# A gated-MLP and linear-attention mixer: residual rows enter the products through a PSUM bank

## The chip, the cores and the metric

The kernel runs on one core of one Trainium2 chip. The time is that of one execution on the device, in microseconds; of several runs the median is given. A core has TensorE (matrix products, which it writes into the eight banks of PSUM), VectorE, ScalarE and GpSimd (elementwise work; GpSimd does not touch PSUM here), and SyncE, which in this kernel issues every DMA. The profile calls them PE, DVE, ACT, POOL and SP; PEld is TensorE's loading of the stationary operand. Each engine works through its own instructions strictly in the order in which the program wrote them, and waits on semaphores for the others. An instruction that waits therefore holds up everything behind it on its engine.

## What is computed

A sequence of 2048 rows of 512 features goes twice through two residual blocks, A and B, with the same weights both times:

```python
x = x + _A_ref(_layernorm(x), A_wqkv, A_wo)      # linear attention, 32 heads of 16
x = x + _B_ref(_layernorm(x), B_w_in, B_w_sp, B_b_sp, B_w_out)   # gated MLP
x = x + _A_ref(_layernorm(x), A_wqkv, A_wo)
x = x + _B_ref(_layernorm(x), B_w_in, B_w_sp, B_b_sp, B_w_out)
```

In block A, `phi(t) = where(t > 0, t + 1, exp(t)) + 1e-6` is applied to queries and keys; `kv = pk^T v`, `z` is the sum of `pk`, and the output is `(pq kv / (pq z + 1e-6)) wo`. In block B, `z = gelu(x w_in)` with 1792 columns; its first half is multiplied by a gate `w_sp layernorm(second half) + b_sp`, where `w_sp` is 2048 x 2048 and mixes the rows; the product with `w_out` comes last. Everything is float32.

## The kernel before

The 2048 rows are cut into 16 tiles of 128 (`NT = 16`). Every float32 operand of a product is split into a high part and the remainder, `split` (L118 on): `high` (L119) copies on ScalarE to the format TensorE takes, `low` (L122) subtracts on VectorE, and `mm3` (L133 to L135) forms high x high, high x low and low x high, so each product of two tiles is three matmuls. A bank is one tile of 128 x 512 float32. Pages (128 x 512 in SBUF) and banks are handed out by `Slots`, first freed first taken; a new owner waits until the old one's last use is done.

One layer (L = 0, then L = 1) is a chain of stages, and each stage writes its engines' order out by hand:

- **P1**, per tile: layer norm, keys and queries, `phi`, and the sums for `kv`. The last six query tiles are put off (`late`, `late_phi`): their products fill TensorE later. `late_phi` ends with three instructions: two on ScalarE (L327, L328) and one on VectorE (L329).
- **transition**: forms the combined matrix W2 of `kv` and `wo`, and prepares the first query tiles.
- **P2**, in steps s = 1 to 18, one tile further in each step. Step s runs on TensorE, in this order: `c(s-1)`, the product of tile s-1 with W2 (12 matmuls); in the first steps transposes and a put-off query product; `e(s-3)`, the second half of the B input product (24 matmuls of 448 columns); and up to two `f` (12 matmuls each), pieces of the first half, which exist from step 6 on, seven for every four tiles. `c2` adds the result to the residual row tile in SBUF (L618) and takes its statistics (L196, L198 on VectorE; L200, L201, L203 on GpSimd). `c3` stores the row tile (L624), normalises it on ScalarE (L209) and stores the normalised tile for the transposed load of a later step. `a`, `a2` scale the query tiles (L565 on GpSimd, L577 to L586 on VectorE; L240 on ScalarE stores the first ones); `b` and `d` turn tiles into stationary operands; `e2` is the GELU on two half banks (L671), `e3`, `e4` its norm; the GELU of `f` is L692. `w1.piece` splits a weight piece, and in the first layer from step 6 on `sums.tick` adds blocks of `w_sp` on GpSimd (L786), from loads that SyncE issues.
- **P4**: 56 steps of the row-mixing product (L906 to L908), whose results are evacuated with bias and gate; then 16 steps `o(i)`, the product with `w_out` (21 matmuls), the addition of the residual tile (L1001) and its store (L1003). `zsplit(i+2)` prepares the operand two steps ahead. In the first layer `join` puts the start of the next P1 between the `o` steps: row loads, three norms (i = 7, 8, 9), and the key and query weights (i = 10 to 13).

The two additions that the change touches are these:

```python
nc.vector.tensor_add(x, x, self.cb)   # L618, in c2
nc.vector.tensor_add(x, x, b)         # L1001, in o
```

Of the kernel before, what the change touches and what calls it, by code (L numbers as in the profile page):

```python
# [49 lines left out]
            self.free_list.append(n)  # L50


class Sheets:


# [16 lines left out]
def mixer_kernel(ctx: ExitStack, tc: tile.TileContext, x_in, wqkv, wo_d, win1_d, win2_d, wsp_d, bsp_d, wout_d,  # L72
# [9 lines left out]
    pages = Slots(main, "pg", 22)  # L82
    quads = Slots(main, "qd", 6)
    bigs = Slots(main, "bg", 4)
    banks = Slots(psum, "bank", 8)

    PAGE = [P, 512]
    ztile = {}
# [29 lines left out]
    def high(h, src):  # L118
        nc.scalar.activation(h, src, AF.Copy)  # L119
# [8 lines left out]
        else:  # L128
            low(l, src, h)

    def mm3(out, a, b, start, stop):
        (ah, al), (bh, bl) = a, b
        nc.tensor.matmul(out, ah, bh, start=start, stop=False)  # L133
        nc.tensor.matmul(out, ah, bl, start=False, stop=False)  # L134
        nc.tensor.matmul(out, al, bh, start=False, stop=stop)  # L135

    class Weight:

# [79 lines left out]
    def transposes(src):  # L218
        b = banks.get([P, 4, P])
        for c in range(4):  # L220
            nc.tensor.transpose(b[:, c, :], src[:, c * P:(c + 1) * P], ident)
        return b

    class Turn:
# [40 lines left out]
    class P1:  # L265
# [123 lines left out]
        def start(self):  # L389

            self.loadx(0)
            self.loadx(1)
            nc.sync.dma_start(ident, ident_d)
            for w in (self.wk, self.wq):
                for _ in range(4):
                    w.fetch()
            self.loadx(2)
            self.loadx(3)
            nc.sync.dma_start(mask, mask_d)
            m, f = pages.get(PAGE, F32R), pages.get(PAGE)  # L400
            nc.vector.memset(f, 1.0)
            nc.vector.tensor_copy(m, f)
            b = banks.get(PAGE)

            def idle(n):
                for _ in range(n):
                    nc.tensor.matmul(b, ones, m, start=True, stop=True)

            idle(10)
            self.ln_a(0)  # L410
            self.ln_a(1)
            self.ln_b(0)
            self.wk.piece()
            self.T_high(0)
            idle(4)
            banks.put(b)
            pages.put(m, f)
            self.T_low(0)
            self.wk.piece()
            self.ln_b(1)  # L420
            self.wk.piece()
            self.wk.piece()
            self.kb[0] = self.proj(0, self.wk, lambda: self.T(1))
            self.ln_a(2)
            for _ in range(4):
                self.wq.piece()
            self.ln_b(2)
# [51 lines left out]
    def transition(p1, p2):  # L479
        wv, wo = p1.wv, p1.wo  # L480
        zh, zl = pages.get(PAGE, F32R), pages.get(PAGE, F32R)
        za = p1.zacc
        nc.vector.tensor_scalar(za, za, NT * PHI_EPS, None, op0=OP.add)
        split(zh, zl, za, True)
        pages.put(za)
        p1.late()
        p1.wk.free()
        g = (quads.get([P, 4, 512], F32R), quads.get([P, 4, 512], F32R))
        for c in range(4):
            split(g[0][:, c, :], g[1][:, c, :], p1.G[c])  # L490
            banks.put(p1.G[c])
        zb = banks.get(PAGE)
        nc.tensor.matmul(zb, ones, zh, start=True, stop=False)
        nc.tensor.matmul(zb, ones, zl, start=False, stop=True)
        pages.put(zh, zl)
        p2.zbc = pages.get(PAGE)
        nc.scalar.activation(feats(p2.zbc, True), feats(zb, False), AF.Copy)
        banks.put(zb)
        p2.a(0)
        p1.late_phi()  # L500
        p2.win1.fetch()
        p2.win1.fetch()
        p2.zeps = small.tile([P, 32], F32, name="zeps", bufs=1)
        nc.vector.tensor_reduce(p2.zeps, p2.zbc.rearrange("p (h d) -> p h d", d=16), axis=mybir.AxisListType.X,
                                op=OP.add)
        nc.vector.tensor_scalar(p2.zeps, p2.zeps, PHI_EPS, PHI_EPS, op0=OP.mult, op1=OP.add)

        p2.a2_den(0)
        m = pages.get([P, 4, P])
        for q in range(4):  # L510
            b = banks.get([P, P])
            s = slice(q * P, (q + 1) * P)
            for c in range(4):
                mm3(b, (wv.h[:, c, s], wv.l[:, c, s]), (g[0][:, c, s], g[1][:, c, s]), c == 0, c == 3)
            nc.vector.tensor_mul(m[:, q, :], b, mask)
            banks.put(b)
        kvh, kvl = pages.get([P, 4, P], F32R), pages.get([P, 4, P], F32R)
        for q in range(0, 4, 2):
            split(kvh[:, q:q + 2, :], kvl[:, q:q + 2, :], m[:, q:q + 2, :])
        pages.put(m)  # L520
        quads.put(*g)
        wv.free()
        p2.a2_mul(0)
        p2.a(1)
        p1.late()
        p2.a2_den(1)
        p2.W2 = (quads.get([P, 4, 512], F32R), quads.get([P, 4, 512], F32R))
        for q in range(4):
            b = banks.get(PAGE)
            mm3(b, (kvh[:, q, :], kvl[:, q, :]), (wo.h[:, q, :], wo.l[:, q, :]), True, True)  # L530
            split(p2.W2[0][:, q, :], p2.W2[1][:, q, :], b)
            banks.put(b)
            if q == 1:
                p2.b(0)
        pages.put(kvh, kvl)
        wo.free()
        p2.a(2)
        p1.late_phi()
        p2.a2_mul(1)
        p1.late()  # L540
        p2.a(3)
        p2.a2(2)
        p1.late_phi()


    class P2:
        def __init__(self, p1):
            self.L = L = p1.L
            self.p1 = p1
            self.win1, self.win2 = w_in1(), p1.win2  # L550
            self.qturn, self.xturn = Turn(f"qt{L}", range(5), True), Turn(f"yt{L}", range(4))
            self.qp, self.qT, self.x, self.ms, self.xB, self.z, self.zms = {}, {}, {}, {}, {}, {}, {}
            self.fq = deque()
            self.fnext = []

        def loadx(self, i):
            if i < NT:
# [43 lines left out]
        def b_low(self, i):  # L601
# [3 lines left out]
            home.put(b)  # L605
            self.qT[i] = (h, l)

        def c(self, i):
            h, l = self.qT.pop(i)
            b = banks.get(PAGE)  # L610
            for g in range(4):
                mm3(b, (h[:, g, :], l[:, g, :]), (self.W2[0][:, g, :], self.W2[1][:, g, :]), g == 0, g == 3)
            pages.put(h, l)
            self.cb = b

        def c2(self, i):
            x = self.x[i]
            nc.vector.tensor_add(x, x, self.cb)  # L618
            banks.put(self.cb)
            self.ms[i] = stats(x, 1)  # L620

        def c3(self, i):
            x = self.x.pop(i)
            nc.sync.dma_start(xs[2 * self.L + 1, i], x)  # L624
            y = pages.get(PAGE)
            turned = self.xturn.turned(i)
            normalise(feats(y, turned), feats(x, False), self.ms.pop(i))
            pages.put(x)
            self.xturn.store(i, y)
            if i in self.xturn.by_pe:  # L630
                self.xB[i] = y
            else:
                pages.put(y)
# [64 lines left out]

        def run(self, sums):
            w1 = self.win1  # L700
            for s in range(1, NT + 3):
                self.loadx(s + 1)
                self.qturn.load(s + 1)
# [39 lines left out]
                if s >= 3:  # L743
                    self.e(s - 3)
                    self.e2(s - 3)
                    self.e3(s - 3)
                self.f()
                self.f()
                self.fq.extend(self.fnext)
# [60 lines left out]
    class P4:  # L810
# [7 lines left out]
        def __init__(self, p2, sums):  # L818
            self.L = p2.L
            self.p2, self.sums = p2, sums  # L820
            self.raw, self.w, self.z, self.z1, self.x, self.zs = {}, {}, {}, {}, {}, {}
            self.steps = [(p, k) for p in self.ORDER for k in range(HT)]
            self.beta = self.delta = None
            self.wout = {}

        def fetch(self, g):
            if g >= len(self.steps):
# [75 lines left out]

        def acc(self, out, h, l, o, w, j, start, stop):
            m = nc.tensor.matmul
            m(out, h[:, o], w[:, 0, j, :], start=start, stop=False, skip_group_check=True)  # L906
            m(out, h[:, o], w[:, 1, j, :], start=False, stop=False, skip_group_check=True)  # L907
            m(out, l[:, o], w[:, 0, j, :], start=False, stop=stop, skip_group_check=True)  # L908
# [76 lines left out]
        def zsplit(self, i):  # L985
# [5 lines left out]
            split(q[:, 0], q[:, 1], src)  # L991
            self.zs[i] = q

        def o(self, i):
            q = self.zs.pop(i)
            b = banks.get(PAGE)
            for f in range(NF):
                mm3(b, (q[:, 0, f, :], q[:, 1, f, :]), self.wout[f], f == 0, f == NF - 1)
            quads.put(q)
            x = self.x.pop(i)  # L1000
            nc.vector.tensor_add(x, x, b)  # L1001
            banks.put(b)
            nc.sync.dma_start(xs[2 * self.L + 2, i], x)  # L1003
            pages.put(x)
# [3 lines left out]
        def run(self, nxt):  # L1008
# [35 lines left out]
                    self.evac(p)  # L1044
            pages.put(*self.bs)
            self.zsplit(1)
            for i in range(NT):
                self.loadx(i + 2)
                self.o(i)
                self.zsplit(i + 2)  # L1050
                if nxt is not None:
# [67 lines left out]
```

## Time and profile before

| | |
|---|---|
| runs | 1406.6, 1407.32, 1407.64 us; median 1407.32 |
| profiled execution | span 1405.0 us from the first to the last instruction |
| TensorE clock granted | 1.000 over the whole span |
| busy PE / DVE / ACT / POOL | 1392.5 / 902.0 / 572.1 / 405.3 us |

The profile is of one execution, with its own span; the runs' median lies 2.3 us above it. In a timeline row stand the start and the length in us, the engine, the line, the operation, the tile written and the tile read (buffer numbers left out), their shapes and the count; in brackets how long the engine sat idle just before and what released it. Neighbouring rows can overlap a little: an instruction begins while the one ahead drains, and the ends of matmuls are modelled. A row of a waits table gives who waited for whom, the total in us, the number of times and the longest. A row of a group gives the shortest, median and longest duration in ns and when the first and the last began.

### The profile page before, as it was taken

What the parts mean: (1) busy time and instruction counts of PE and PEld (TensorE: products, weight loads), DVE (VectorE), ACT (ScalarE), POOL (GpSimd) and SP (SyncE); (2) the same over time, 40 slices, a digit from 0 to 9 for tenths busy, and PEclk for the clock granted to TensorE, in tenths of its full rate; (3) what the DMA queues carried; (4) which work ended last, traced back from release to release, by engine and by line L of the source; (5) the groups of instructions that cost most, each with busy time, mean ns of one, the idle gap of its engine ahead of it and who ended that gap; (6) DMA issues with size and microseconds to landing.
All of it is one profiled execution on the core that took longest, in us unless ns stands there. A gap on an engine that the chain in (4) does not pass through costs nothing.

```text
span 1405.0 us, 17478 instructions
## 1 busy us (share of the span) xinstructions
PE 1392.5 (99%) x6270; PEld 1161.3 (83%) x6270; DVE 902.0 (64%) x1275; ACT 572.1 (41%) x871; POOL 405.3 (29%) x490
## 2 busy tenths in 40 slices
PE   9999999999999999999999999999999999999998
PEld 7777888888888888888888888888888888888887
DVE  7887786763577665583578867766415466665632
ACT  5665544443332332341357655444333233333420
POOL 3643245544356001041024434432100030022300
PEclk9999999999999999999999999999999999999999
DMA  6742157876897444453645412554335344434432
GB/s 198 236 147 68 53 183 232 267 240 203 309 323 265 129 121 141 159 179 105 225 128 159 127 45 96 179 177 163 114 119 158 105 165 134 130 122 167 152 112 90
DMA packets 142454, 225.68 MB, mean 161 GB/s; under 512 B 11936, under 2 KB 50592, under 8 KB 142368
## 3 DMA queue, kind: packets, MB, share of 16 engines
q1 hardware_dynamic: 142368, 224.57, 49.3%
q8 instruction: 49, 0.80, 0.2%
q14 instruction: 37, 0.30, 0.1%
HBM read 156.63 MB, written 67.90 MB: 160 GB/s over the span
## 4 chain that ended last, share of the span: by engine, by line
PE 77%; DVE 3%; ACT 2%; issue 1%; DMA 1%; POOL 0%; SPq 0%; DVEq 0%; POOLq 0%; ACTq 0%
PE bank L907 13%; PE bank L906 13%; PE bank L908 13%; PE bank L135 13%; PE bank L134 13%; PE bank L133 13%; DVE pg L260 1%; DMA pg<-in_x_dram 1%; DVE pg L341 0%; DVE pg L329 0%; ACT pg L328 0%; ACT pg L327 0%; DVE bg L122 0%; ACT z_q L328 0%; ACT z_q L327 0%
## 5 line engine op out<-in xcount | busy, mean ns | idle before, releaser
L906 PE MATMUL bank<-qd,pg 128*128 128x512 f32 x800 | 311.2, 389 | 0.0
L908 PE MATMUL bank<-qd,pg 128*128 128x512 f32 x800 | 311.2, 389 | 0.0
L907 PE MATMUL bank<-qd,pg 128*128 128x512 f32 x800 | 311.2, 389 | 0.0
L845 DVE TENSOR_TENSOR qd<-qd,qd 128x1024 fp32r<-128x1024 f32 x112 | 153.9, 1374 | 176.7 <-ACT qd L844 176.5
L844 ACT ACTIVATE qd<-qd 128x1024 fp32r<-128x1024 f32 x112 | 118.5, 1058 | 215.7 <-PE bank L908 198.9
L933 POOL TENSOR_TENSOR bg<-bg,pg 128x512 f32<-128x512 f32 x56 | 85.5, 1563 | 409.6 <-DVE bg L960 195.5
L906 PEld LDWEIGHTS bank<-qd,pg 128*128 128x128 f32 x800 | 150.1, 188 | 31.6
L908 PEld LDWEIGHTS bank<-qd,pg 128*128 128x128 f32 x800 | 150.2, 188 | 31.1
L907 PEld LDWEIGHTS bank<-qd,pg 128*128 128x128 f32 x800 | 150.2, 188 | 31.0
L135 PE MATMUL bank<-qd,pg 128*128 128x512 f32 x384 | 150.7, 392 | 2.7 <-DVE pg L122 2.5
L200 POOL TENSOR_SCALAR rs<-mv 128x1 f32<-128x1 f32 x96 | 36.1, 376 | 391.5 <-DVE mv L198 363.6
L209 ACT ACTIVATE pg<-pg,nb,rs 128x512 f32<-128x512 f32 x63 | 51.1, 811 | 181.8 <-POOL nb L203 181.7
L133 PE MATMUL bank<-qd,pg 128*128 128x512 f32 x288 | 112.5, 391 | 1.4 <-ACT pg L119 1.4
L134 PE MATMUL bank<-qd,pg 128*128 128x512 f32 x288 | 112.3, 390 | 0.0
L786 POOL TENSOR_TENSOR pg<-pg,pg 128x512 f32<-128x512 f32 x56 | 80.6, 1439 | 49.1 <-DMA pg<-in_wsp_dram 38.7
L133 PE MATMUL bank<-bg,qd 128*128 128x448 f32 x256 | 94.2, 368 | 0.0
L135 PE MATMUL bank<-bg,qd 128*128 128x448 f32 x256 | 93.7, 366 | 0.1
L134 PE MATMUL bank<-bg,qd 128*128 128x448 f32 x256 | 93.6, 366 | 0.0
L135 PEld LDWEIGHTS bank<-qd,pg 128*128 128x128 f32 x384 | 72.0, 188 | 21.2 <-DVE pg L122 6.5
L135 PE MATMUL bank<-qd,bg 128*128 128x512 f32 x224 | 87.4, 390 | 0.0
L134 PE MATMUL bank<-qd,bg 128*128 128x512 f32 x224 | 87.4, 390 | 0.0
L133 PE MATMUL bank<-qd,bg 128*128 128x512 f32 x224 | 87.2, 390 | 0.0
(128 smaller groups left out, 2630.4 us busy)
## 6 DMA issues: line engine op xcount, KB each, us to landing
qd<-s SPq DMA_DIRECT2D x64, 512.0 KB, 3.4
qd<-in_wsp_dram SPq DMA_DIRECT2D x48, 512.0 KB, 3.8
pg<-x SPq DMA_DIRECT2D x64, 256.0 KB, 3.1
z<-pg SPq DMA_DIRECT2D x56, 256.0 KB, 2.5
pg<-in_wsp_dram SPq DMA_DIRECT2D x56, 256.0 KB, 5.1
s<-pg SPq DMA_DIRECT2D x56, 256.0 KB, 5.1
pg<-z SPq DMA_DIRECT2D x56, 256.0 KB, 5.2
x<-pg SPq DMA_DIRECT2D x48, 256.0 KB, 2.6
```

Source lines behind the costliest of these rows:

```text
L133: nc.tensor.matmul(out, ah, bh, start=start, stop=False)
L134: nc.tensor.matmul(out, ah, bl, start=False, stop=False)
L135: nc.tensor.matmul(out, al, bh, start=False, stop=stop)
L200: nc.gpsimd.tensor_scalar(rs, mv[:, 1:2], LN_EPS, None, op0=OP.add)
L209: nc.scalar.activation(y, x, AF.Identity, bias=nb, scale=rs)
L786: nc.gpsimd.tensor_tensor(t, a, b, op=OP.add)
L844: nc.scalar.activation(w[:, 0], r, AF.Copy)
L845: nc.vector.tensor_sub(w[:, 1], r, w[:, 0].bitcast(F32))
L906: m(out, h[:, o], w[:, 0, j, :], start=start, stop=False, skip_group_check=True)
L907: m(out, h[:, o], w[:, 1, j, :], start=False, stop=False, skip_group_check=True)
L908: m(out, l[:, o], w[:, 0, j, :], start=False, stop=stop, skip_group_check=True)
L933: nc.gpsimd.tensor_tensor(u, u, z1, op=OP.mult)
```

## The change

Before a residual product begins, ScalarE copies the tile of residual rows into a bank (`seed`). The product's first matmul no longer starts the bank afresh (`start=False`), so all matmuls add onto the rows. In P2, `c2` takes the statistics from the bank, `c3` normalises from the bank and then copies the bank back into the row tile on ScalarE, before the tile's store is issued, which moves behind the normalisation. In P4, `o` copies the finished bank into the row tile on ScalarE instead of adding on VectorE.

The seed of P2's tile s is written into ScalarE's order in step s, behind the GELU of `e2(s-3)` and ahead of those of `f`; the seed of tile 0 stands ahead of step 1. In P4 the seed of tile i+1 stands ahead of `o(i)`. A new class `Banks` records how many columns of each bank the last fresh product covered (transposes record 0), and `seeded` takes the first free bank on which a product of that width will add rather than overwrite.

```diff
+class Banks(Slots):
+    def __init__(self, pool, prefix, n):
+        super().__init__(pool, prefix, n)
+        self.adds = [0] * n
+    def started(self, t, columns):
+        self.adds[self.held[id(t)][0]] = columns
+    def seeded(self, shape):
+        for n in self.free_list:
+            if self.adds[n] >= shape[-1]:
+                self.free_list.remove(n)
+                self.free_list.appendleft(n)
+                return self.get(shape)
+        return None
...
-    banks = Slots(psum, "bank", 8)
+    banks = Banks(psum, "bank", 8)
...
-    def mm3(out, a, b, start, stop):
+    def mm3(out, a, b, start, stop, shared=False):
...
+        if start:
+            banks.started(out, out.shape[-1])
...
+        def seed(self, i):
+            if i >= NT:
+                return
+            b = self.cb[i] = banks.seeded(PAGE)
+            high(b, self.x[i])
+
         def c(self, i):
             h, l = self.qT.pop(i)
-            b = banks.get(PAGE)
             for g in range(4):
-                mm3(b, (h[:, g, :], l[:, g, :]), (self.W2[0][:, g, :], self.W2[1][:, g, :]), g == 0, g == 3)
+                mm3(self.cb[i], (h[:, g, :], l[:, g, :]), (self.W2[0][:, g, :], self.W2[1][:, g, :]), False, g == 3,
+                    True)
             pages.put(h, l)
-            self.cb = b
 
         def c2(self, i):
-            x = self.x[i]
-            nc.vector.tensor_add(x, x, self.cb)
-            banks.put(self.cb)
-            self.ms[i] = stats(x, 1)
+            self.ms[i] = stats(self.cb[i], 1)
 
         def c3(self, i):
-            x = self.x.pop(i)
-            nc.sync.dma_start(xs[2 * self.L + 1, i], x)
+            x, b = self.x.pop(i), self.cb.pop(i)
             y = pages.get(PAGE)
             turned = self.xturn.turned(i)
-            normalise(feats(y, turned), feats(x, False), self.ms.pop(i))
+            normalise(feats(y, turned), feats(b, False), self.ms.pop(i))
+            high(x, b)
+            banks.put(b)
+            nc.sync.dma_start(xs[2 * self.L + 1, i], x)
             pages.put(x)
...
         def run(self, sums):
             w1 = self.win1
+            self.seed(0)
             for s in range(1, NT + 3):
...
                     self.e3(s - 3)
+                self.seed(s)
                 self.f()
                 self.f()
...
+        def seed(self, i):
+            if i >= NT:
+                return
+            b = self.ob[i] = banks.seeded(PAGE)
+            high(b, self.x[i])
+
         def o(self, i):
             q = self.zs.pop(i)
-            b = banks.get(PAGE)
+            x, b = self.x.pop(i), self.ob.pop(i)
             for f in range(NF):
-                mm3(b, (q[:, 0, f, :], q[:, 1, f, :]), self.wout[f], f == 0, f == NF - 1)
+                mm3(b, (q[:, 0, f, :], q[:, 1, f, :]), self.wout[f], False, f == NF - 1, True)
             quads.put(q)
-            x = self.x.pop(i)
-            nc.vector.tensor_add(x, x, b)
+            high(x, b)
             banks.put(b)
...
             self.zsplit(1)
+            self.seed(0)
             for i in range(NT):
                 self.loadx(i + 2)
+                self.seed(i + 1)
                 self.o(i)
```

More of the change, by code (lines that the diff above doesn't have):

```diff
@@ L129, in split @@
             low(l, src, h)
-    def mm3(out, a, b, start, stop):
+    def mm3(out, a, b, start, stop, shared=False):
         (ah, al), (bh, bl) = a, b
-        nc.tensor.matmul(out, ah, bh, start=start, stop=False)
-        nc.tensor.matmul(out, ah, bl, start=False, stop=False)
-        nc.tensor.matmul(out, al, bh, start=False, stop=stop)
+        nc.tensor.matmul(out, ah, bh, start=start, stop=False, skip_group_check=shared)
+        nc.tensor.matmul(out, ah, bl, start=False, stop=False, skip_group_check=shared)
+        nc.tensor.matmul(out, al, bh, start=False, stop=stop, skip_group_check=shared)
+        if start:
+            banks.started(out, out.shape[-1])
     class Weight:
@@ L221, in transposes @@
             nc.tensor.transpose(b[:, c, :], src[:, c * P:(c + 1) * P], ident)
+        banks.started(b, 0)
         return b
@@ L415, in start @@
             idle(4)
+            banks.started(b, 512)
             banks.put(b)
@@ L494, in transition @@
         nc.tensor.matmul(zb, ones, zl, start=False, stop=True)
+        banks.started(zb, 512)
         pages.put(zh, zl)
@@ L554, in __init__ @@
             self.fnext = []
+            self.cb = {}
         def loadx(self, i):
@@ L823, in __init__ @@
             self.beta = self.delta = None
-            self.wout = {}
+            self.wout, self.ob = {}, {}
         def fetch(self, g):
@@ L905, in acc @@
             m = nc.tensor.matmul
+            if start:
+                banks.started(out, 512)
             m(out, h[:, o], w[:, 0, j, :], start=start, stop=False, skip_group_check=True)
```

## The prediction

> **What bounds the kernel now.** I read the page's busy line first, then TensorE's table of waits, then the timelines of each engine where the two changed products run.
>
> ```profile
> span 1405.0 us, 17478 instructions
> PE 1392.5 (99%) x6270; PEld 1161.3 (83%) x6270; DVE 902.0 (64%) x1275; ACT 572.1 (41%) x871; POOL 405.3 (29%) x490
> PE bank L135 <- DVE pg L122: 2.5, 4, 0.7
> ```
>
> TensorE is busy for all but 12.5 of 1405.0 us, so its queue is the bound, and the change takes no matmul from it. There is little to win: of its waits, the only one near the change is 2.5 us behind `low` (L122). What matters is whether TensorE must newly wait. The starts of `c(0)` to `c(5)`, the attention output products of the first P2, on TensorE:
>
> ```profile
> 149.64 0.39 PE L133 MATMUL bank<-qd,pg 128*128 128x512 f32 x1
> 152.36 0.60 PE L221 MATMUL bank<-ident,pg 128*128 128x128 f32 x4
> 155.55 0.39 PE L133 MATMUL bank<-qd,pg 128*128 128x512 f32 x1
> 162.92 0.39 PE L133 MATMUL bank<-qd,pg 128*128 128x512 f32 x1
> 172.25 0.40 PE L133 MATMUL bank<-qd,pg 128*128 128x512 f32 x1
> 180.74 0.39 PE L133 MATMUL bank<-qd,pg 128*128 128x512 f32 x1
> 188.86 0.40 PE L133 MATMUL bank<-qd,pg 128*128 128x512 f32 x1
> ```
>
> `c` lasts 2.72 us (149.64 to 152.36); the early steps last 5.91, 7.37, 9.33, 8.49 and 8.12 us. ScalarE in the same stretch:
>
> ```profile
> 152.75 0.58 ACT L327 ACTIVATE z_q<-bank 128x512 f32<-128x512 f32 x1
> 153.36 0.63 ACT L328 ACTIVATE z_q<-z_q 128x512 f32<-128x512 f32 x1
> 153.90 0.58 ACT L119 ACTIVATE pg<-bank 128x512 fp32r<-128x512 f32 x1
> 157.62 0.82 ACT L209 ACTIVATE pg<-pg,nb,rs 128x512 f32<-128x512 f32 x1 [3.14 <-POOL nb L203]
> 159.42 0.64 ACT L240 ACTIVATE pg<-pg 128x512 f32<-128x512 f32 x1 [0.98 <-DVE pg L586]
> 159.96 0.57 ACT L327 ACTIVATE z_q<-bank 128x512 f32<-128x512 f32 x1
> 160.57 0.63 ACT L328 ACTIVATE z_q<-z_q 128x512 f32<-128x512 f32 x1
> 174.78 0.98 ACT L671 ACTIVATE z_z<-bank 128x448 f32<-128x448 f32 x2
> 182.45 0.95 ACT L671 ACTIVATE z_z<-bank 128x448 f32<-128x448 f32 x2
> 191.20 0.82 ACT L209 ACTIVATE pg<-pg,nb,rs 128x512 f32<-128x512 f32 x1 [4.65 <-POOL nb L203]
> 192.95 0.95 ACT L671 ACTIVATE z_z<-bank 128x448 f32<-128x448 f32 x2
> 847.38 0.63 ACT L328 ACTIVATE z_q<-z_q 128x512 f32<-128x512 f32 x1
> ```
>
> The reader is to see that ScalarE runs late: the work it does for step 1 (157.62 to 161.20) ends after TensorE has begun step 2 (155.55). Today nothing on TensorE needs that work soon.
>
> **The change, part by part.** *Removed:* 64 residual adds on VectorE.
>
> ```profile
> L618 DVE TENSOR_TENSOR pg<-pg,bank x32: 640/675/689, 154.6 to 1010.9; 128x512 f32<-128x512 f32 x32
> 156.07 0.18 DVE L198 BATCH_NORM_AGGREGATE mv<-st 128x2 f32<-128x6 f32 x1
> 156.35 0.22 POOL L200 TENSOR_SCALAR rs<-mv 128x1 f32<-128x1 f32 x1 [14.86 <-DVE mv L198]
> 157.32 0.27 POOL L203 TENSOR_SCALAR nb<-mv,rs 128x1 f32<-128x1 f32 x1
> 158.07 1.32 DVE L586 SCALAR_TENSOR_TENSOR pg<-z_q,den 128x512 f32<-128x512 f32 x1
> ```
>
> 32 x 0.675 us here and as many in P4 leave an engine 64% busy; what this gives TensorE is at most the 2.5 us of waits on `low`, queued behind that add. *Added:* 64 seeds and 64 copies back on ScalarE. No row shows ScalarE writing a bank, so a seed is bounded by its 128x512 rows: 0.57 (L327) to 0.82 us (L209). I take 0.6, nearest the plain copies (0.58); back to back they step 0.55, since neighbouring rows overlap by 0.09 (153.99 to 153.90); normalise then counts 0.72. Twelve exposed seeds at 0.82 would add 2.6 us.
>
> [...]
>
> *Statistics and normalise on the bank:* one bank operand instead of one page operand, same shapes; the rows that read a bank (0.57 to 0.58) are no longer than those that read a page (0.63), so 0. *Store of x moved behind normalise and copy back:* on SP's queue the y store behind it goes out about 0.55 (copy) + 0.5 (issue) later. Its reader is the transposed load, used a step later; a step of 8 to 13 us hides 1.05. Without that cover it is a delay of each step, priced under the second rival. *Banks:* one more is held for about a step of eight, and `seeded` takes one free for long: 0.
>
> *The new wait* carries the sum: `c(i)` cannot begin before seed(i), queued on ScalarE behind all of step i's normalise, store, phi and GELU; and what stands behind the seed (the `f` GELUs, the weight copy) is not needed sooner.
>
> - seed(0) stands behind the last `late_phi`, which ends at 153.99. It ends at 154.5, so `c(0)` starts at 154.55 instead of 149.64: **+4.9**.
> - Step 1: `c(0)` ends 157.3; statistics without the add reach the aggregate at 158.1. From there to the end of L586 it was 3.3 us (156.07 to 159.39); `low(1)` now waits for its transposes behind `c(0)`, +0.3: 161.75. POOL's 1.25, normalise and copy back (0.72 + 0.55) fit in before. L240 to the end of L328 is 1.78: 163.55; then the seed. `c(1)` at 164.0 instead of 155.55: **+8.45** in all.
> - Step 2: the same chain of 9.45 with d(0)'s transposes and one more VectorE `low`, +0.8: `c(2)` at 174.25, **+11.3**.
> - Steps 3 and 4: no `f` follows `e`. The seed waits for the second GELU half, which waits for the end of `e`: 8.49 of TensorE work + 0.1 + half a pair of GELUs 0.55 + seed 0.6 = 9.75 each. `c(4)` at 193.75, **+13.0**.
> - Step 5: from the end of step 4's GELUs to normalise it was 7.8 (183.40 to 191.20), less 0.67 for the add; from normalise to the end of the GELUs 2.7 (191.20 to 193.90), plus copy back 0.55 and seed 0.55. From 193.1 that makes `c(5)` 204.1 instead of 188.86: **+15.2**.
>
> The second layer starts the same way at the same spacing (the `exp` ahead of its first seed stands at 847.38, 694.02 after the first layer's), so **2 x 15.2 = 30.4**. From step 6 two `f` products follow `e`, and TensorE covers the chain. In the second layer, between two `c` starts:
>
> ```profile
> 945.47 0.39 PE L133 MATMUL bank<-qd,pg 128*128 128x512 f32 x1
> 951.73 0.82 ACT L209 ACTIVATE pg<-pg,nb,rs 128x512 f32<-128x512 f32 x1 [4.94 <-POOL nb L203]
> 954.00 0.95 ACT L671 ACTIVATE z_z<-bank 128x448 f32<-128x448 f32 x2
> 958.52 0.39 PE L133 MATMUL bank<-qd,pg 128*128 128x512 f32 x1
> ```
>
> GELUs end at +9.48; less 0.7 for the add, plus 0.55 and 0.55, the seed ends at +9.9 of a 13.05 us step: hidden with 3 us to spare. In steps with one `f` (13.05 - 2.72 = 10.33) it just fits; I give the four of them **0.7** together. In the first layer alone, the first matrix sums of step 6 wait for loads that SP issues behind the stores of that step's `f`:
>
> ```profile
> 206.32 1.93 SPq L115 DMA_DIRECT2D pg<-in_wsp_dram  x4
> 212.42 2.65 POOL L786 TENSOR_TENSOR pg<-pg,pg 128x512 f32<-128x512 f32 x2 [3.94 <-DMA pg<-in_wsp_dram]
> ```
>
> The second `f` now ends at +13.05 of the step, its GELU and first store at +14.3; 6.1 later (206.32 to 212.42) come the adds, 2.65 long, then POOL's 1.25 for `c(6)` and from normalise to the seed's end 3.2 + 1.1: +28.6 against the 26.1 at which TensorE wants `c(7)`: **+2.5**.
>
> P4, first layer, where the next P1's norms are joined:
>
> ```profile
> 669.82 0.69 DVE L1001 TENSOR_TENSOR pg<-pg,bank 128x512 f32<-128x512 f32 x1 [3.07 <-PE bank L135]
> 671.42 0.68 DVE L196 BATCH_NORM_STATS2 st<-pg 128x6 f32<-128x512 f32 x1
> 673.69 0.82 ACT L209 ACTIVATE pg<-pg,nb,rs 128x512 f32<-128x512 f32 x1 [21.96 <-POOL nb L203]
> 674.57 0.69 DVE L1001 TENSOR_TENSOR pg<-pg,bank 128x512 f32<-128x512 f32 x1 [2.25 <-PE bank L135]
> 686.39 2.07 SPq L115 DMA_DIRECT2D pg<-in_wqkv_dram  x4
> 691.02 0.63 ACT L119 ACTIVATE qd<-pg 128x512 fp32r<-128x512 f32 x1 [5.23 <-DMA pg<-in_wqkv_dram]
> ```
>
> An `o` takes 4.75 us (669.82 to 674.57). In front of seed(i+2) after `o(i)` now stand the copy back (0.6), the split's copy of 128x896 (about 0.95, by elements from the 128x512 row) and the join's work: alone 2.2, hidden. With a norm: copy 0.6, split copy 0.95, its VectorE `low` (0.9, from the end of L1001 at 670.51 to 671.42), then the chain from statistics to normalise, 671.42 to 673.69 = 2.27, normalise 0.72, seed 0.6, hand-overs 0.15: 6.2. For i = 7 that is 1.45 over; for 8 and 9, whose chain begins right behind the seed before, 1.15 each. At i = 10 the join's copy waits for loads issued behind the x store: 4.63 from issue to use (686.39 to 691.02) after about 1.4 of copy back and issues, then 1.15 for copy and seed, less 4.75: 2.4. Together **+6.2**. The second layer's P4 has no join: 0. The tail changes an add of 0.69 into a copy of 0.6: **-0.1**.
>
> Sum: 30.4 + 0.7 + 2.5 + 6.2 - 0.1 = **39.7 us** on a profiled span of 1405.0. That span lies 2.3 below the runs' median of 1407.32, so the run becomes 1407.3 + 39.7 = **1447** (+2.8%).
>
> **The rivals.** *The TensorE clock drops in the new stalls.* The forecast idles TensorE for about 4.9, 3.3 and 4.1 us at the start of each P2, longer than any wait in this trace after its start. What a slow TensorE looks like stands at the start:
>
> ```profile
> 2.31 4.11 PE L407 MATMUL bank<-pg,ones 128*128 128x512 f32 x10 [2.31 <-DVE pg L402]
> ```
>
> Ten matmuls in 4.11 us, 0.41 each, against 12 in 2.72, 0.227 each; the page's granted clock still reads full there. A relapse costs 10 x 0.18 = 1.8 us; four make 7.3: **1454**. Nothing in the trace shows a relapse, so 0.17. [...]
>
> *The ScalarE chain becomes the period in the first layer's middle.* There VectorE and POOL also work for the sums, and the x page and the y page come free later. At +1.05 per step and nothing hidden in steps 6 to 15, 10 us more: **1457**. Against it: the chain has 3 us to spare once ScalarE waits for TensorE. 0.13.
>
> *Only the relief of VectorE counts.* If every seed were done before TensorE asks, the four waits on `low` (2.5 us) would go and nothing come: **1404.8**, no change by this kernel's measure (0.2%). The place is seed(0): it decides if ScalarE ends the last `late_phi` before 149.6. The rows say 153.99, by the order of its own queue. 0.04; a partial exposure (P4's joins hidden, about 1440) lies inside the forecast.
>
> **How the numbers follow.** Forecast 0.66, clock 0.17, chain 0.13, relief 0.04. The forecast alone: 1436 to 1452 (P4's 6.2 and the sums' 2.5 away, or seeds at 0.82 and 2 to 3 us of longer chains). The range 1431 to 1463 adds both slower rivals and chains 15% shorter. Faster by over 0.2%: 0.02; within: 0.03; slower: 0.95.
>
> **What would show it.** On TensorE: waits released by ScalarE's copy into a bank ahead of `c(0)` to `c(5)`, about 5, 3.5, 4, 1.2, 1.2, 2.5 us in each layer; almost none from `c(8)` on; a few of 1 to 2 us at the ninth to twelfth `o` of the first P4 and none in the second. VectorE about 43 us less busy, ScalarE about 77 more (128 x 0.6). Wrong if ScalarE's early seeds end before TensorE arrives, if `c` starts without them, or if waits persist through the steps with two `f`.

## The result and the profile after

The changed kernel takes 1455.76 us (median of 4 runs, 1455.05 to 1459.02), the kernel before 1407.48 us in the same comparison (4 runs, 1406.6 to 1407.88): a ratio of 1.0349, interval 1.0337 to 1.0361. It is 3.5% slower. The forecast was 1447, the range 1431 to 1463.

In the changed kernel's lines, `high` is L138, `low` L141, `mm3` L152 to L154, the normalisation L230, the transposes L242. The page of the changed kernel, its span, its busy line, its line of granted clock (one digit for each fortieth of the span), and the costliest form of the product's first matmul:

```profile
span 1453.8 us, 17527 instructions
PE 1406.6 (97%) x6270; PEld 1169.4 (80%) x6270; DVE 853.7 (59%) x1211; ACT 637.7 (44%) x999; POOL 405.7 (28%) x490
PEclk9999799999999999999999998999999999999999
L152 PE MATMUL bank<-qd,pg 128*128 128x512 f32 x288 | 118.4, 411 | 33.3 <-ACT bank L138 31.7
```

TensorE issues the same 6270 matmuls and is busy 14.1 us longer (1406.6 against 1392.5); the rest of the 48.8 us by which the span grew is idle time. VectorE is 48.3 us less busy and ScalarE 65.6 us more, against the 43 and 77 of the forecast. (The 128 added copies last 76.0 us one by one; busy time counts the overlap of neighbouring rows only once.) TensorE's table of waits, two rows:

```profile
PE bank L152 <- ACT bank L138: 36.9, 15, 4.7
PE bank L154 <- DVE pg L141: 0.6, 1, 0.6
```

Fifteen times TensorE waits for ScalarE's copy into a bank, 36.9 us in all; the waits on `low` shrank from 2.5 to 0.6. That is 35.0 us more idle, and with the 14.1 us of busy time 49.1, against the 48.8 by which the span grew. The waits on TensorE's timeline, in the first layer's P2, then c(0) to c(2) of the second, then `o(9)` to `o(11)` of the first P4:

```profile
155.06 0.80 PE L152 MATMUL bank<-qd,pg 128*128 128x512 f32 x1 [4.72 <-ACT bank L138]
155.66 0.63 PE L153 MATMUL bank<-qd,pg 128*128 128x512 f32 x1
156.09 0.63 PE L154 MATMUL bank<-qd,pg 128*128 128x512 f32 x1
...
159.93 0.60 PE L242 MATMUL bank<-ident,pg 128*128 128x128 f32 x4
...
167.12 0.80 PE L152 MATMUL bank<-qd,pg 128*128 128x512 f32 x1 [3.85 <-ACT bank L138]
...
179.68 0.62 PE L152 MATMUL bank<-qd,pg 128*128 128x512 f32 x1 [3.13 <-ACT bank L138]
...
191.16 0.50 PE L152 MATMUL bank<-qd,pg 128*128 128x512 f32 x1 [1.13 <-ACT bank L138]
...
201.05 0.50 PE L152 MATMUL bank<-qd,pg 128*128 128x512 f32 x1 [1.13 <-ACT bank L138]
...
211.18 0.50 PE L152 MATMUL bank<-qd,pg 128*128 128x512 f32 x1 [1.77 <-ACT bank L138]
...
698.05 0.50 PE L152 MATMUL bank<-wo,qd 128*128 128x512 f32 x1 [1.43 <-ACT bank L138]
...
704.01 0.50 PE L152 MATMUL bank<-wo,qd 128*128 128x512 f32 x1 [0.91 <-ACT bank L138]
...
711.86 0.50 PE L152 MATMUL bank<-wo,qd 128*128 128x512 f32 x1 [2.79 <-ACT bank L138]
...
877.70 0.79 PE L152 MATMUL bank<-qd,pg 128*128 128x512 f32 x1 [4.73 <-ACT bank L138]
...
890.22 0.79 PE L152 MATMUL bank<-qd,pg 128*128 128x512 f32 x1 [3.87 <-ACT bank L138]
...
901.71 0.50 PE L152 MATMUL bank<-qd,pg 128*128 128x512 f32 x1 [3.43 <-ACT bank L138]
...
902.98 0.39 PE L154 MATMUL bank<-qd,pg 128*128 128x512 f32 x1
903.21 0.39 PE L152 MATMUL bank<-qd,pg 128*128 128x512 f32 x1
```

Two things are to be seen. The brackets are the new waits. And behind `c(0)`'s wait the matmuls start 0.43 us apart (155.66 to 156.09), behind `c(2)`'s in the second layer 0.23 (902.98 to 903.21): `c(0)` now lasts 4.87 us (155.06 to 159.93) where it lasted 2.72. The stretches of the changed kernel's trace (busy time of PE, PEld, DVE, ACT, POOL with their counts; the column before the last two is the granted clock) say why:

```profile
152.00:160.00 8.00, 4.93 (x13) 3.87 (x14) 1.34 (x2) 2.23 (x4) 0.00 (x0) 0.57 0.00 0
160.00:170.00 10.00, 6.15 (x24) 4.73 (x23) 5.05 (x8) 4.64 (x8) 3.57 (x5) 0.81 0.25 79
170.00:180.00 10.00, 6.87 (x28) 5.31 (x27) 4.79 (x9) 4.96 (x9) 2.32 (x4) 0.84 0.23 79
872.00:885.00 13.00, 8.27 (x28) 6.26 (x27) 5.41 (x11) 3.49 (x7) 0.69 (x2) 0.74 0.00 0
```

The clock was granted in full everywhere in the kernel before; here it falls six times: behind `c(0)`, `c(1)`, `c(2)` in the first layer, `c(0)`, `c(1)` in the second, and `o(11)` in the first P4. The two kernels issue the same matmuls in the same order, so the step from each start to the next, less the idle time, can be compared one by one. Of the 14.1 us, 12.3 lie in steps at half clock: some 50 matmuls that start 0.43 instead of 0.23 us after the one ahead, and longer first steps and transposes beside them. Another 1.2 are first steps behind waits that ran at full clock, ten of the fifteen (0.34 instead of 0.23 us). The last 0.7 us is spread over the trace.

### The profile page after: what moved, and what is told of

Same layout as the page of the kernel before. It is cut to its first block, busy times and chain, and to the rows that moved or that the text cites. A ratio compares the mean times of both kernels' runs of the same rounds, so it can differ in the third digit from the quotient of the medians.

```text
span 1453.8 us, 17527 instructions
## 1 busy us (share of the span) xinstructions
PE 1406.6 (97%) x6270; PEld 1169.4 (80%) x6270; DVE 853.7 (59%) x1211; ACT 637.7 (44%) x999; POOL 405.7 (28%) x490
## 4 chain that ended last, share of the span: by engine, by line
PE 81%; ACT 7%; DVE 7%; issue 2%; DMA 2%; POOL 1%; SPq 0%; DVEq 0%; ACTq 0%; POOLq 0%
PE bank L152 14%; PE bank L153 14%; PE bank L154 14%; PE bank L940 12%; PE bank L941 12%; PE bank L939 12%; DVE pg L282 1%; DVE pg L351 1%; ACT pg L230 1%; DVE pg L363 1%; ACT pg L350 1%; ACT z_q L350 1%; ACT pg L349 1%; DVE bg L141 1%; ACT z_q L349 1%
## 5 line engine op out<-in xcount | busy, mean ns | idle before, releaser
L939 PEld LDWEIGHTS bank<-qd,pg 128*128 128x128 f32 x800 | 150.1, 188 | 31.4
L940 PEld LDWEIGHTS bank<-qd,pg 128*128 128x128 f32 x800 | 150.2, 188 | 31.1
L941 PEld LDWEIGHTS bank<-qd,pg 128*128 128x128 f32 x800 | 150.1, 188 | 31.1
L154 PE MATMUL bank<-qd,pg 128*128 128x512 f32 x384 | 153.8, 400 | 0.7 <-DVE pg L141 0.6
L152 PE MATMUL bank<-qd,pg 128*128 128x512 f32 x288 | 118.4, 411 | 33.3 <-ACT bank L138 31.7
L138 ACT ACTIVATE pg<-bank 128x512 f32<-128x512 f32 (+1 forms) x77 | 45.6, 592 | 127.3 <-PE bank L154 91.5
L152 PEld LDWEIGHTS bank<-qd,pg 128*128 128x128 f32 x288 | 56.4, 196 | 50.7 <-ACT bank L138 37.3
L141 DVE TENSOR_TENSOR qd<-bg,qd 128x896 fp32r<-128x896 f32 x32 | 35.8, 1117 | 103.1 <-ACT qd L138 103.1
L152 PE MATMUL bank<-bg,qd 128*128 128x448 f32 x256 | 94.0, 367 | 0.0
L154 PE MATMUL bank<-bg,qd 128*128 128x448 f32 x256 | 93.4, 365 | 0.0
L152 PE MATMUL bank<-wo,qd 128*128 128x512 f32 x224 | 88.1, 394 | 5.1 <-ACT bank L138 5.1
L154 PEld LDWEIGHTS bank<-qd,pg 128*128 128x128 f32 x384 | 74.4, 194 | 18.3 <-DVE pg L141 2.4
```

What stands on the lines that cost most here:

```text
L141: nc.vector.tensor_sub(l, src, h.bitcast(F32))
L152: nc.tensor.matmul(out, ah, bh, start=start, stop=False, skip_group_check=shared)
L154: nc.tensor.matmul(out, al, bh, start=False, stop=stop, skip_group_check=shared)
```

## The experiments

Theory: the seed's place in ScalarE's queue makes TensorE wait (forecast), and the waits cost a second time through the clock (first rival). Other theories: ScalarE's added work costs by itself; the price lies in P4.

**Which product carries it.** Two kernels, each with one half of the change.

```diff
 # p2_only: o(i) and its loop as before; c, c2, c3 as changed
 # p4_only: c, c2, c3 and their loop as before; o(i) as changed
```

> The seeds of P2 alone; P4 adds on VectorE as before. If the time went to TensorE waiting for P2's early seeds and to the slow matmuls behind those waits, this keeps nearly all of it: the changed kernel's 1455.8 us less the 5.1 us of waits at the first P4's o steps, 1450.5 us (1449 to 1452). If P4's copies back cost more than those waits show, it is clearly lower, 1440 or less.

> The seeds of P4 alone; P2 as before. By the waits at three o steps of the first P4 (1.4, 0.9, 2.8 us): 1407.5 + 5.1 = 1412.5 us (1411.5 to 1414), and none of it in the second layer's P4, which has no join. If the copies back on ScalarE cost by themselves, about 0.6 us for each of 32 tiles, it would be 1420 us or more.

The first product alone took 1453.88 us (1447.56 to 1454.05; ratio 1.0316, 1.0293 to 1.0339), the output product alone 1413.75 (ratio 1.0042, 1.0027 to 1.0057). TensorE's waits, of the first:

```profile
PE bank L152 <- ACT bank L138: 31.6, 12, 4.7
```

and of the second:

```profile
PE bank L152 <- ACT bank L138: 4.8, 3, 2.4
```

The twelve waits are `c(0)` to `c(5)` in two layers, the three are `o(9)` to `o(11)`. Both halves came out above the expected 1450.5 and 1412.5 us, by 3.4 and 1.3 us, and together they cost 53.0 us where the whole change costs 48.3. The number of falls of the clock differs: the trace of the first half has seven in P2, that of the changed kernel five.

**The clock by itself.** The same kernel as the changed one, but TensorE does useless matmuls while it would wait.

```diff
         def c(self, i):
+            if i < 3:
+                self.fill((18, 14, 14)[i])   # matmuls into a bank that nobody reads
```

> The changed kernel with 18, 14 and 14 extra matmuls on spare data ahead of c(0), c(1) and c(2) of each layer, into a bank that nothing reads; they run while TensorE waits for the seed. If the slow matmuls (0.43 us apart instead of 0.23) come of the clock after an idle stretch, they go: c(0) to c(3) take about 29.7 us in each layer instead of 36.1 and 33.9, and the time is about 1445 us (1443 to 1448) with a granted clock near 1.00. If they are slow because they add onto a bank that ScalarE wrote, or share a port with it, nothing changes: 1455 us or, with the extra work, more.

It took 1445.7 us (1444.76 to 1447.95; ratio 1.0271, 1.0256 to 1.0286): 10.1 us faster than the changed kernel, with 92 matmuls more. Its timeline and its stretch around `c(0)`:

```profile
149.52 4.24 PE L642 MATMUL bank<-qd 128*128 128x512 f32 x18
154.41 0.50 PE L152 MATMUL bank<-qd,pg 128*128 128x512 f32 x1 [0.64 <-ACT bank L138]
```

```profile
155.00:165.00 10.00, 9.31 (x43) 7.40 (x42) 5.06 (x8) 4.66 (x8) 2.30 (x4) 1.00 0.22 79
```

`c(0)` still starts at 154.4 and not at 149.6, so the wait is there, filled; the clock is full. `c(0)` to `c(5)` start at 154.41, 164.50, 174.58, 184.46, 194.34 and 204.48 us. The 10.1 us is the share of the clock; the 12.3 counted above are of one execution, and the four runs of each of the two kernels spread over 4.0 and 3.2 us. What is left, 1445.7 - 1407.3 = 38.4 us, is the waits and the restarts behind them.

**ScalarE's work without the wait.** The kernel before, with all 128 additional ScalarE copies at their places, the seeds into a bank that nobody reads and the copies back into a spare page; VectorE still adds.

```diff
         def c2(self, i):
             nc.vector.tensor_add(x, x, self.cb)
...
             normalise(feats(y, turned), feats(x, False), self.ms.pop(i))
+            g = pages.get(PAGE)
+            high(g, self.cb)
...
+                self.seed(s)
```

> The kernel before, with all of ScalarE's added work and none of the new order on TensorE: at each place of a seed ScalarE copies the rows into a bank that nothing reads, at each place of a copy back it copies the product's bank into a spare page; the products start afresh and VectorE still adds. If the cost is the wait for the seed, the time stays near 1407.5 us (1406 to 1411) with ScalarE some 77 us busier. If it is ScalarE's 128 extra copies by themselves, or their access to the banks, it is about that of the changed kernel, 1450 us.

1417.56 us (ratio 1.0069, 1.0052 to 1.0086): a miss, 10 us above the kernel before. Its waits and the longest of them:

```profile
PE bank L133 <- ACT qd L119: 3.6, 5, 1.9
```

```profile
695.51 0.50 PE L133 MATMUL bank<-wo,qd 128*128 128x512 f32 x1 [1.87 <-ACT qd L119]
```

No product waits for a seed, but the copies hold up others of ScalarE's work: the high parts of operands (`qd`) come late five times, and behind the last, in the first P4, the clock falls once more. Compared step by step with the kernel before, TensorE is idle for 5.1 us more, the slow stretch costs 1.6 and the first steps behind waits 1.2; some 2 of the 10.2 us by which the span grew are not explained. So ScalarE's work is not free where its place in the queue is ahead of an operand. Whether it costs anywhere else, the next runs tell.

**The seeds one tile earlier.** In P2 seed(s+1) in step s, the first two ahead of the last `late_phi`; in P4 seed(i+2) right behind the copy back of `o(i)`. One kernel does both, one only P2.

```diff
+        p2.seed(0)
+        p2.seed(1)
         p1.late_phi()
...
-            self.seed(0)
...
-                self.seed(s)
+                self.seed(s + 1)
...
+            self.seed(1)             # this and the next two only in the first of the two kernels
...
-                self.seed(i + 1)
                 self.o(i)
+                self.seed(i + 2)
                 self.zsplit(i + 2)
```

> The changed kernel with every seed one tile earlier in ScalarE's order: P2's seeds of tiles 0 and 1 in the transition, ahead of the second put-off phi, then the seed of tile s+1 in step s; P4's seed of tile i+2 right behind the copy back of o(i), ahead of the split and the join. All work of the change is kept. If the wait for late seeds (and the clock behind it) is the whole cost, the waits by ScalarE's copy into a bank vanish, VectorE's relief takes back some of the 2.5 us of waits on its low parts, and the time is about 1405 us (1404 to 1409), no slower than before. If statistics, normalise and copies on the bank cost by themselves, it stays above 1420.

> The same with P4's seeds left where the change has them. Expected: the 5.1 us of waits at the first P4 return, about 1410 us (1409 to 1414); the difference to the run before prices P4's place alone.

Both early: 1425.56 us (ratio 1.0123, 1.0105 to 1.0141), far from the expectation. P2 alone early: 1415.97 (ratio 1.0059, 1.0043 to 1.0075), at 2 us above its range. On ScalarE, in the kernel with both, two neighbouring instructions:

```profile
695.85 0.60 ACT L138 ACTIVATE bank<-pg 128x512 f32<-128x512 f32 x1 [6.76 <-DMA pg<-x]
696.39 0.94 ACT L138 ACTIVATE qd<-bg 128x896 fp32r<-128x896 f32 x1
```

and on its TensorE:

```profile
697.38 0.80 PE L152 MATMUL bank<-wo,qd 128*128 128x512 f32 x1 [6.07 <-ACT qd L138]
```

A seed put earlier asks for the residual row earlier. This one sat 6.76 us at the head of ScalarE's queue waiting for the row's load, the split behind it came late, and TensorE waited 6.07 us for the split. The wait was moved from one operand to another.

**P2 early, P4 as before.** This asks whether place in the queue is all that the change costs in P2.

```diff
 # as the kernel with P2 early; o(i) adds on VectorE again, no seeds in P4
```

> The first product with its seeds one tile earlier (as in the run with the first product's seeds early), the output product as in the kernel before. In that earlier run the stalls of the first product were gone but for 0.90, 0.62 and 0.90 us, against 0.72, 0.56, 0.72 and 0.55 us before, so if place in ScalarE's queue is all that the change costs there, 1407.5 us (1406 to 1409.5). If ScalarE's added work costs by itself what the run with the work and without the wait lost, shared evenly between the two products, 1411 to 1413. If the freed VectorE shortens anything, under 1405.

1408.26 us (10 runs, 1407.39 to 1410.88), against 1407.33 (19 runs): ratio 1.0009, interval 1.0 to 1.0019. The busy line of its page, and two rows of its TensorE's waits:

```profile
PE 1393.2 (99%) x6270; PEld 1162.0 (83%) x6270; DVE 878.2 (62%) x1243; ACT 603.0 (43%) x935; POOL 406.9 (29%) x490
```

```profile
PE bank L152 <- ACT qd L138: 1.9, 1, 1.9
PE bank L154 <- DVE pg L141: 1.8, 2, 0.9
```

There is no row for a copy into a bank any more. ScalarE does all 64 added copies of P2, VectorE is 23.8 us less busy, and TensorE's time is what it was. Some 46 us of the 48 of the change are the place of P2's seeds in one queue. What the relief of VectorE gives is not seen by itself: the waits on `low` shrink from 2.5 to 1.8 us, a new wait of 1.9 us on an operand of ScalarE's (`qd`) stands against it, and the net is no gain.

**P4's seeds out of the way.** The seed of tile i+2 behind the split of tile i+2 and ahead of what `join` issues; in a second kernel the residual row is also loaded one tile earlier. P2 early in both.

```diff
-                self.loadx(i + 2)
-                self.seed(i + 1)
+                self.loadx(i + 2)        # second kernel: i + 3
                 self.o(i)
                 self.zsplit(i + 2)
+                self.seed(i + 2)
```

> Both seeds off the path: the first product's one tile earlier, the output product's tile i+2 seeded behind the split of tile i+2 and ahead of what the next layer puts in, so that no normalisation stands between a seed and its product and no load held by a seed stands ahead of a split. Place in the queue as the whole cost: the three stalls of 1.44, 0.91 and 2.42 us at the first output product go, and with the last one its half-clock stretch of some 1.9 us; from 1415.97 us that gives 1409.3 (1407 to 1411). If a seed that waits for its residual load only moves the stall (it held ScalarE 6.76 us when it stood ahead of the split), a wait of 2 us or more on a ScalarE copy stays and the time is 1413 to 1418.

> As the run with the seed behind the split, with the residual row of the output product loaded one tile earlier as well. If the residual's load is what is late, this is the fastest of the three with no wait on ScalarE at the first output product: 1408.5 us (1406.5 to 1411). If the load was not late there, no difference from that run beyond 1 us. If the third residual page starves another tile of pages, a wait on a load appears and the time is over 1412.

The first took 1414.74 us (ratio 1.0056, 1.0041 to 1.0071), the second 1410.15 (ratio 1.0022, 1.0013 to 1.0032). In the first the seed's load moved the stall, as its second expectation had it; ScalarE there:

```profile
689.01 0.60 ACT L138 ACTIVATE bank<-pg 128x512 f32<-128x512 f32 x1 [6.07 <-DMA pg<-x]
```

TensorE waited 4.20 us behind it. With the load one tile earlier that is gone, and what is late next shows; ScalarE and TensorE of the second kernel:

```profile
693.91 0.63 ACT L138 ACTIVATE qd<-pg 128x512 fp32r<-128x512 f32 x1 [3.81 <-DMA pg<-in_wqkv_dram]
...
696.40 0.50 PE L152 MATMUL bank<-wo,qd 128*128 128x512 f32 x1 [1.75 <-ACT bank L138]
```

The join's copy of a weight piece waits 3.81 us for its load, the seed stands behind it, and TensorE idles 1.75 us. No version with seeds was faster than the kernel before.

**How short a wait costs the clock.** The rows of P4 had shown half clock behind waits of 1.75 to 2.8 us. So the full fill was cut, to leave idle time of that length ahead of `c(0)` to `c(2)`.

```diff
-                self.fill((18, 14, 14)[i])
+                self.fill((9, 6, 4)[i])      # fill_half;  (13, 9, 8) in fill_most
```

> The change with 9, 6 and 4 matmuls into an unread bank ahead of c(0), c(1) and c(2) of each layer, in place of 18, 14 and 14. Waits and fill together are as long as with the full fill, so all time above that run's 1445.7 us is clock. The remaining idle is 2.65, 2.5 and 2.5 us (the full fill's remainder plus 9, 8 and 10 matmuls of 0.2275 us). Theory A, half clock only after some 3 us of idle or more: no relapse in P2 and 1445.7 (1444.5 to 1447.5). Theory B, idle of 1.75 to 2.8 us is enough when its phase is bad, as the rows of the first output product in four kernels suggest: two to six relapses of some 1.9 us in P2, 1449 to 1457.

> As before with 13, 9 and 8 matmuls: idle of 1.75, 1.8 and 1.6 us remains ahead of c(0), c(1) and c(2). Theory A: 1445.7 us (1444.5 to 1447.5). Theory B: between the full and the half fill, up to four relapses, 1446 to 1452; the waits of 1.71 to 1.77 us at c(5) in the changed kernel left the clock full, so fewer relapses than with the half fill.

1449.92 us (1446.79 to 1453.22; ratio 1.0291, 1.0274 to 1.0309) and 1447.82 us (1446.79 to 1450.39; ratio 1.0287, 1.0271 to 1.0302): above the 1445.7 of the full fill though the same time is waited or filled. The intervals of the three ratios overlap, so the times alone do not decide; the granted clock does. It was 0.998 to 0.999 in the four runs of the full fill and 0.993 to 0.997 in those of the half fill. In P2, where no wait of the two kernels is longer than 2.7 us, the traces show four falls with the half fill, three with the larger one and none with the full fill: theory B holds. TensorE's timeline of the first, and its stretches around those rows (why they are cut at these times is told in the last section):

```profile
154.51 0.80 PE L152 MATMUL bank<-qd,pg 128*128 128x512 f32 x1 [2.69 <-ACT bank L138]
...
178.72 0.50 PE L152 MATMUL bank<-qd,pg 128*128 128x512 f32 x1 [2.52 <-ACT bank L138]
```

```profile
150.38:153.79 3.41, 1.44 (x7) 0.86 (x5) 1.62 (x4) 2.08 (x4) 0.00 (x0) 1.00 0.00 0
153.79:157.21 3.42, 2.69 (x6) 2.17 (x7) 0.69 (x1) 0.67 (x2) 0.00 (x0) 0.50 0.00 0
174.27:177.69 3.42, 1.92 (x9) 1.27 (x7) 1.99 (x4) 2.25 (x5) 0.93 (x1) 1.00 0.46 135
177.69:181.10 3.41, 2.38 (x10) 1.99 (x11) 0.69 (x1) 1.53 (x3) 1.29 (x1) 1.00 0.28 100
```

Half clock came behind 2.69 us of idle and not behind 2.52: of the first wait 1.97 us lie in one stretch of 3.41 us, of the second 1.50 and 1.03 us in two.

## Why the prediction was right, and where it was not

The sign, the place and the mechanism were right. The time came out 8.8 us above the forecast because one rival happened beside it; the stated range had room for that. Term by term:

- *The waits at `c(0)` to `c(5)`.* The forecast named about 5, 3.5, 4, 1.2, 1.2 and 2.5 us; measured were 4.72, 3.85, 3.13, 1.13, 1.13, 1.77 in the first layer and 4.73, 3.87, 3.43 at the start of the second. The forecast's 30.4 us for both layers stands against 15.7 + 16.0 of waits less the 1.9 saved on `low`: 29.8. The per-step chain that set them (GELU half, normalise, copy back, seed) was read correctly from the rows of before. The kernel with the stalls filled, where the clock stays full, shows it best: `c(1)`, `c(2)`, `c(4)` and `c(5)` start at 164.50, 174.58, 194.34 and 204.48 us, and the forecast put them at 164.0, 174.25, 193.75 and 204.1. (The six waits that the forecast lists as signs come to 17.4 us a layer, its own starts move by 15.2; the measured 15.7 and 16.0 lie nearer the starts.)
- *The clock in the new stalls* is what the forecast left out of its sum. It was a rival at 0.17 with 4 events of 1.8 us, 7.3 in all; that there would be four was the author's estimate, which no run shows. It came six times and cost 10 to 12 us (10.1 by the full fill, 12.3 counted in one trace). The forecast's reason, that nothing in the trace shows a relapse, was worth little: after its start the longest wait in the trace of before is 1.36 us (at 41.24 us), and the shortest that half clock followed, in the traces counted in the last section, is 1.75 us. (Nor does the full clock that its page gives for the slow first matmuls say anything: that trace's first record of the clock begins at 5.65 us.) Forecast 39.7 and clock 10.1 would be 49.8; measured 48.3. That these lie so close is in part luck, as the next terms show: 3.2 us of the sum did not come, the waits were 1.7 us shorter than forecast, and the slow first steps behind the waits, 1.2 us at full clock, were in no term.
- *The first layer's sums at step 7, 2.5 us*, did not come. The chain was as described up to the loads, but these took less time. On SP, POOL, ScalarE and TensorE of the changed kernel:

```profile
225.59 1.83 SPq L134 DMA_DIRECT2D pg<-in_wsp_dram  x4
...
229.45 2.66 POOL L817 TENSOR_TENSOR pg<-pg,pg 128x512 f32<-128x512 f32 x2 [2.40 <-DMA pg<-in_wsp_dram]
...
237.03 0.61 ACT L138 ACTIVATE bank<-pg 128x512 f32<-128x512 f32 x1
...
237.69 0.50 PE L152 MATMUL bank<-qd,pg 128*128 128x512 f32 x1
```

  From issue to the adds it was 3.9 us and not the 6.1 taken from the kernel before. The seed ends at 237.64 and `c(7)` starts at 237.69: the step was on the edge, and the term was mis-sized by the length of one load.
- *The one-`f` steps, 0.7 us:* no wait there; the term was 0.
- *The first P4, 6.2 us:* 1.43 + 0.91 + 2.79 = 5.1 at three `o` products, not four. The forecast gave 1.45, 1.15, 1.15 and then 2.4 for the weight load ahead of `o(12)`. The third was larger because the residual row of tile 11 was late, not a norm:

```profile
711.21 0.60 ACT L138 ACTIVATE bank<-pg 128x512 f32<-128x512 f32 x1 [1.77 <-DMA pg<-x]
```

  That delay gave the weights time to land, so the fourth wait vanished. In the kernel with the stalls filled the third wait was 0.44 us shorter, and 0.58 us of the fourth was there at `o(12)`; in the kernel with the row loaded earlier the same load cost 1.75 us, at `o(13)`.
- *Seeds at 0.6 us; statistics and normalise from a bank at no more than from a page.* In P2 the normalisation took 0.779 us from the bank (median) where it had taken 0.817 from the page, the statistics 0.698 where they had taken 0.694. The groups of ScalarE's copies in the changed kernel (shortest, median, longest in ns):

```profile
L138 ACT ACTIVATE bank<-pg x64: 578/592/618, 154.4 to 1441.7; 128x512 f32<-128x512 f32 x64
L138 ACT ACTIVATE pg<-pg x77: 418/623/635, 18.0 to 1044.5; 128x512 fp32r<-128x512 f32 x73, 128x256 fp32r<-128x256 f32 x4
```

  Copies into a bank took 0.592 us, those from page to page 0.623, 5% more. The second group also converts its output, but the ten copies from page to page that do not (L262) took 0.629 us. The 64 copies back from a bank to a page took 0.591 us, so here a copy is as much shorter when the bank is what it reads.
- *The rivals.* ScalarE's chain as the period of the middle steps did not come (no wait at `c(6)` or later). The relief of VectorE came in busy time, but brought no gain in time: the kernel with only P2's seeds, all early, is 0.9 us slower than the kernel before.

## What to carry to other kernels

Before moving work to a less busy engine, find what stands ahead of it in that engine's queue and what stands behind: the 64 added copies of P2 cost 46 us in one place and 0.9 us one tile earlier, and a copy put earlier can itself wait for a load and hold up the next operand. Price a new wait on a saturated TensorE as the wait plus the half clock that may follow it: here 10 to 12 us for six falls, so some 1.7 to 2 us each, behind waits of 2.79 to 4.73 us in the changed kernel; in the kernels with a partial fill half clock followed waits of 1.77 to 2.69 us, and in the one with the row loaded earlier a wait of 1.75. That the trace of before shows no such relapse says nothing when it holds no such wait.

## What the runs showed that had not been expected

Half clock came behind shorter waits than the 3 us or so of theory A. In six traces (the kernel before, the changed kernel, the two partial fills, the two with P4's seeds out of the way), counted on TensorE's timelines from 100 to 270 and from 640 to 960 us for products of 448 or 512 columns: none of 30 waits of 0.81 to 1.72 us was followed by half clock; 12 of 17 between 1.75 and 3.43 us were; and all 5 of 3.85 us or more. The length alone does not sort them: 3.43 us in the second layer of the changed kernel left the clock full, 1.75 us in the kernel with the row loaded earlier did not, as that trace's stretches show:

```profile
694.04:697.45 3.41, 1.66 (x7) 0.85 (x6) 2.25 (x3) 3.41 (x7) 0.00 (x0) 1.00 0.80 278
697.45:700.86 3.41, 3.41 (x10) 2.63 (x9) 2.86 (x5) 2.85 (x5) 0.00 (x0) 0.50 0.72 255
```

In the changed kernel's trace the granted clock falls at 152.60, 166.25, 179.90, 712.38, 876.22 and 889.88 us, each time for 3.41 or 6.83 us; all these falls, and the rises behind them, lie whole multiples of 3.4133 us apart. The stretches of 3.41 us above, of two other traces, are cut at changes of the granted clock and in steps of that length from there. In the changed kernel's trace, cut in the same way, TensorE was idle for 66 to 100% of the stretch ahead of each of the six falls. No other stretch at full clock from 20 to 1440 us was idle for more than 54%, and that one, 896.70 to 900.12 us, at the wait of 3.43 us, ended in no fall. In the stretches shown, 58% (150.38 to 153.79 us, half fill) and 51% (694.04 to 697.45 us, row loaded earlier) ended in a fall, 44% (174.27 to 177.69 us, half fill) did not. The shares rest on ends of matmuls that are modelled, and why the clock stayed full behind 54% and fell behind 51% is not shown.

Left open: what the relief of VectorE gives by itself, some 2 us of the kernel with ScalarE's work and no wait, and the one stretch that was idle for 54% without a fall.
